# The second product turned: weights stationary, 512 tokens moving, output through 32x32 transposes

## The chip, the cores and the metric

The kernel runs on one core of one Trainium2 chip. A core has a matrix engine (TensorE, PE in the profile), a vector engine (VectorE, DVE), an activation engine (ScalarE, ACT), a general engine (GpSimd, POOL), a queue engine that here only issues transfers (SyncE, SP), and 16 DMA engines that the queues share. The metric is the device time of one execution in microseconds (us). Before the change, three runs took 592.19, 592.72 and 592.80 us; the median is 592.72 us.

## The reference, cut to what matters

There are two stages. The first is an attention block with 32 inducing points: for each of 4 batches of 12,480 tokens of width 128, the 32 points attend to the tokens and give `h` (32 x 128), and then every token attends to the 32 rows of `h`. The second is a two-layer network on the result, with a leaky unit between the layers whose slope is given per hidden channel.

```python
def mab(q, kv):
    s = scale * (q @ kv.transpose(0, 2, 1))
    s = s - s.max(-1, keepdims=True)
    a = np.exp(s)
    a /= a.sum(-1, keepdims=True) + 1e-09
    return a @ kv
h = mab(I, x)            # 4 x 32 x 128
x = mab(x, h)            # 4 x 12480 x 128
h = x @ w_in             # 49920 x 2048
g = np.maximum(h, 0.0) + alpha * np.minimum(h, 0.0)
out = g @ w_out          # 49920 x 128
```

## The kernel before, in words

The kernel never forms the attention output. For a batch it computes `hW = h @ w_in` once (32 x 2048). The hidden layer of a token is then `hW` weighted by the token's 32 exponentials, divided by their sum; since the leaky unit commutes with a positive factor, the division is left to the very end. The leaky unit is written as alpha times its input, which is linear, plus (1 - alpha) times the positive part. The linear part is folded into a 32 x 128 matrix `hA` per batch, and `W1` is `w_out` scaled by (1 - alpha).

*Groups and steps.* Tokens are worked in groups of 512 (`GRP`), four groups (`NQ`) to a stretch of 2,048 tokens, six stretches (`NS`) and a short group of 192 to a batch: 25 groups a batch, 100 in all. A group has four steps `j` (the short group two). In a step `fill` (L424) makes four matmuls, each with 32 rows of `hW` as weights and 512 columns of `rep` (the exponentials) moving; the four use different row groups of the array. Each writes one of six PSUM banks (`ring`). The four banks are evicted with a ReLU to `gt` in bf16 by ScalarE (L448) or VectorE (L450). Which engine takes which bank is fixed in advance by `make_plan` (L703), a beam search over a simple cost model, with 57 ns for each matmul of 128 columns. One step later `mm2` (L454) multiplies: for each bank and each of its four blocks of 128 tokens, a matmul has the block of `gt` as weights (128 x 128) and the matching 128 columns of `W1` moving, and adds to one of two accumulators `acc` (tokens on partitions, channels in the free dimension). The linear part is added to the accumulators of two groups at a time by `linear` (L479), eight matmuls of 128 columns with `rep` as weights.

*Output.* After a group's last step `finish` (L491) multiplies the accumulator with the reciprocal of each token's sum of exponentials (`rd`; one value per partition and block) on VectorE, from PSUM into `ob`, and stores `ob` with one DMA from the GpSimd queue (L516; the last groups from SP). Tokens are laid out so that each partition stores 2 KB in a row. `ob` has three buffers.

*What feeds it.* `b_scores` (L355) computes a stretch's exponentials `e2` (32 inducing points x 4 groups on 128 partitions) and stores them to DRAM (`e2d`); `b_rep` (L374) loads them back four times, as `rep`, on the partitions that `fill` reads. `b_den` (L394) sums them by four matmuls with `pick` and takes the reciprocal `rd`. For the next batch, `a_load` (L122) loads x with a cast to bf16 from the GpSimd queue, `a_xpose` (L140) transposes it into `xT` by a DMA transpose from SP, `a_scores` (L263) computes the scores of the inducing points, and their exponentials `e1` go through a second DMA transpose (`e1T`) to `a_accum`.

*What sets the order.* Every instruction is pinned to program order on its engine (`pin`). Beside the steps of the groups, side work is put in slots (group, step) by `at` (from L654): for a stretch `s`, `b_scores` four groups ahead of its first group, `b_rep` three and `b_den` two groups ahead; for the next batch, a load every two groups, its transpose three groups later and its scores five groups later. DMA issues wait on their queue in program order too, so a waiting issue on SP or GpSimd holds up all that follow there.

Of the kernel before, what the change touches and what calls it, by code (L numbers as in the profile page):

```python
# [25 lines left out]
def kernel(  # L26
# [50 lines left out]
    head_pool = ctx.enter_context(tc.tile_pool(name="headp", bufs=3))  # L77
    rep_pool = ctx.enter_context(tc.tile_pool(name="repp", bufs=3))
    dram = ctx.enter_context(
        tc.tile_pool(name="e2d", bufs=3, space=bass.MemoryType.DRAM)  # L80
    )
    ob_pool = ctx.enter_context(tc.tile_pool(name="obp", bufs=3))
# [4 lines left out]
    accs = [psum.tile([P, NB, C], f32, name=f"acc{i}") for i in range(2)]  # L87
# [14 lines left out]
    def new_batch(b):  # L102
# [11 lines left out]
        st.rden = {}  # L114
        if b > 0:
            st.es = work.tile([P, NS + 1], f32, name="es", tag="es")
            st.hacc = work.tile([P, C], f32, name="hacc", tag="hacc")
            nc.vector.memset(st.es[:], 0.0)
            nc.vector.memset(st.hacc[:], 0.0)
# [102 lines left out]
    def warm(st, n=1):  # L222
        for _ in range(n):
            mm(
                accs[0][:, 1:, :].rearrange("p k c -> p (k c)"), ident[:],
# [128 lines left out]

    def b_scores(st, s):  # L355
        ps = bank()
        if s < NS:
            for q in range(NQ):
                mm(ps[32 * q : 32 * q + 32, :], st.hT, st.xT[:, s, q, :])
            e2 = work.tile([P, GRP], bf16, name="e2", tag="e2")  # L360
            pin(nc.scalar.activation(out=e2[:], in_=ps[:], func=EXP, scale=scale_of(st)))  # L361
            w = GRP
        else:
            mm(ps[0:M, :REM], st.hT, st.xTr[:].rearrange("c j p -> c (j p)"))
            e2 = work.tile([M, REM], bf16, name="e2r", tag="e2r")
            pin(nc.scalar.activation(out=e2[:], in_=ps[0:M, :REM], func=EXP, scale=scale_of(st, M)))
            w = REM
# [16 lines left out]
    def b_scores_pe(st, q):  # L384
        if q == 0:
            st.rep0 = rep_pool.tile([P, NQ, GRP], bf16, name="rep", tag="rep")
        ps = bank()
        mm(ps[:], st.hT4[:], st.xT[:, 0, q, :])
        pin(nc.scalar.activation(
            out=st.rep0[:, q, :], in_=ps[:], func=EXP, scale=scale_of(st)  # L390
# [3 lines left out]
    def b_den(st, s):  # L394
        e2 = st.e2.pop(s)
        ps = bank()
        if s < NS:
            for j in range(NB):
                mm(ps[:, j * NQ : (j + 1) * NQ], e2[:, j * P : (j + 1) * P], pick[:])
            rd = work.tile([P, NB, NQ], f32, name="rd", tag="rd")  # L400
            pin(nc.vector.reciprocal(
                out=rd[:].rearrange("p j q -> p (j q)"), in_=ps[:, : NB * NQ]
            ))
        else:
            for j in range(JR):
                mm(ps[:PR, j : j + 1], e2[:, j * PR : (j + 1) * PR], pick[0:M, 0:1])
            rd = work.tile([PR, JR, 1], f32, name="rdr", tag="rdr")
            pin(nc.vector.reciprocal(
                out=rd[:].rearrange("p j q -> p (j q)"), in_=ps[:PR, :JR]
            ))  # L410
        st.rden[s] = rd


# [40 lines left out]
    def mm2(st, g, j, gt):  # L454
        pp, nb, cp = shape_of(g)
        acc = accs[(st.b * NG + g) % 2]
        begun = (g % 2 == 1 and st.b + g > 1) or cp > 1
        for r in range(4):
            for i in range(cp):
                c = r * NJ + j * cp + i  # L460
                for k in range(nb):
                    k0 = (i * nb + k) * pp
                    mm(
                        acc[:pp, k, :], gt[:, r, k0 : k0 + pp], W1[:, c, :],
                        start=(j == 0 and r == 0 and i == 0 and k == 0 and not begun),
                        stop=False, skip_group_check=True,
                    )
# [11 lines left out]
    def linear(st, groups):  # L479
        for k in range(NB):  # L480
            for r, g in enumerate(groups):
                pp, nb, cp = shape_of(g)
                if k < nb:
                    mm(
                        accs[(st.b * NG + g) % 2][:pp, k, :],
                        st.rep[g][32 * r : 32 * r + 32, k * pp : (k + 1) * pp],
                        st.hA[32 * r : 32 * r + 32, :],
                        start=((r == 1 or cp > 1) and k == 0), stop=False, skip_group_check=True,
                    )

    def finish(st, g):  # L491
        pp, nb, _ = shape_of(g)
        acc = accs[(st.b * NG + g) % 2]
# [321 lines left out]
```

## Time and profile before

| | |
|---|---|
| median of three runs | 592.72 us |
| span of the profiled execution (first to last instruction) | 591.0 us |
| own time of the profiled execution | not listed beside its span; the median is 1.7 us above the span |
| TensorE busy | 578.7 us (98%) |
| VectorE busy | 517.7 us (88%) |
| ScalarE busy | 502.5 us (85%) |
| GpSimd busy | 84.9 us (14%) |
| DMA packets | 81,825, 70.10 MB, 119 GB/s over the span |
| second product, matmuls of 128 x 128 x 128 | 6,144, mean 220 ns from start to modelled end |
| output multiply on VectorE, 128 x 512 | 96, 681 ns |
| granted TensorE clock | 1.00 |

How to read it: a row of a group names the line of the code, the engine, the operation, output<-inputs, shape and count, then busy time and mean duration. Busy times of TensorE are made from modelled ends of pipelined matmuls, so 98% does not say that it streams 98% of the time; the starts in the timeline do. A timeline row gives the start, the duration of a run of like instructions and their number, and in brackets how long the engine was idle before and what ended it. In the views by stretch, each engine's busy time is followed by its number of instructions, and the last three numbers are the granted clock, the busy share of the 16 DMA engines and GB/s. Time of a GpSimd or SP transfer issue is the issue alone; the landing is listed apart.

### The profile page before, as it was taken

The page shows a single profiled execution, that of the slowest core. Times are in us where ns is not written, and L with a number is a line of the kernel's source. Part 1 is how long each engine was busy: PE and PEld are TensorE (multiplying, and loading weights), DVE is VectorE, ACT ScalarE, POOL GpSimd, SP SyncE. Part 2 cuts the span into 40 slices and gives each one's busy share as a digit, 9 for nine tenths or more (in the row PEclk, how much of TensorE's full clock was granted, in tenths as well). Part 3 has the DMA queues.
Part 4 walks back from the last instruction along what each step waited for, and adds up shares of the span by engine and source line. Part 5 has one row for each costly group of instructions (what it writes and reads, how often), then busy time and mean ns, then how long its engine had stood idle before and what let it go on. Part 6 is the DMA issues. An engine that isn't in the chain of part 4 may idle for free.

```text
span 591.0 us, 21769 instructions
## 1 busy us (share of the span) xinstructions
PE 578.7 (98%) x9218; PEld 434.2 (73%) x9219; DVE 517.7 (88%) x869; ACT 502.5 (85%) x988; POOL 84.9 (14%) x170
## 2 busy tenths in 40 slices
PE   5999999999999999999999999999999999999997
PEld 4677777777777777777777777777777777777776
DVE  3688998999889989998989899988988998998996
ACT  2579888888889988888888998888888988989987
POOL 6631111101011111110111111101101101101100
PEclk9999999999999999999999999999999999999999
DMA  9973978751237569953126597985122221221211
GB/s 198 210 174 90 177 149 163 154 140 55 86 87 165 125 128 185 171 137 92 60 83 142 121 163 129 185 159 131 59 70 80 89 93 54 92 91 56 94 47 62
DMA packets 81825, 70.10 MB, mean 119 GB/s; under 512 B 55440, under 2 KB 71072, under 8 KB 81728
## 3 DMA queue, kind: packets, MB, share of 16 engines
q0 software_dynamic: 12528, 38.51, 26.0%
q1 hardware_dynamic: 69056, 29.68, 25.0%
q8 instruction: 72, 1.18, 0.8%
q10 hardware_dynamic: 144, 0.52, 0.2%
q14 instruction: 25, 0.20, 0.1%
HBM read 40.20 MB, written 28.75 MB: 117 GB/s over the span
## 4 chain that ended last, share of the span: by engine, by line
PE 97%; DVE 1%; DMA 1%; ACT 1%; issue 0%; SPq 0%
PE acc L96 68%; PE ring L96 27%; PE ring L172 1%; DMA ind_f<-in_inducing_dram 1%; ACT gt L448 0%; DVE xT L178 0%; DVE gt L450 0%; DVE ob L503 0%; DVE xn L612 0%; ACT xT L180 0%; SPq L526 0%; ACT ob L507 0%; DVE hT L246 0%; DVE ind_b L562 0%; PE ring L565 0%
## 5 line engine op out<-in xcount | busy, mean ns | idle before, releaser
L448 ACT ACTIVATE gt<-ring 128x512 bf16<-128x512 f32 x899 | 469.5, 599 | 67.8 <-ACT gt L448 27.4
L450 DVE TENSOR_SCALAR gt<-ring 128x512 bf16<-128x512 f32 x669 | 435.1, 685 | 52.2 <-PE ring L96 37.8
L96 PE MATMUL acc<-W,gt 128*128 128x128 bf16 x6272 | 417.9, 220 | 0.2 <-DVE ob L503 0.2
L96 PEld LDWEIGHTS <-gt 128*128 128x128 bf16 x6272 | 352.4, 98 | 79.6 <-issue 76.8
L96 PE MATMUL ring<-rep,hW 32*128 32x512 bf16 (+1 forms) x1600 | 157.3, 379 | 0.0
L516 POOL DMA_DIRECT2D out_dram<-ob x96 | 51.8, 540 | 476.5 <-DVE ob L503 412.6
L96 PEld LDWEIGHTS <-hW 32*128 32x128 bf16 x1600 | 41.1, 91 | 41.6 <-issue 0.5
L503 DVE TENSOR_TENSOR ob<-acc,rd 128x512 f32<-128x512 f32 x96 | 65.4, 681 | 2.5 <-PE acc L96 2.5
L96 PE MATMUL acc<-hA,rep 32*128 32x128 bf16 x392 | 19.8, 214 | 0.0
L96 PEld LDWEIGHTS <-rep 32*128 32x128 bf16 x392 | 15.6, 93 | 5.6
L129 POOL DMA_DIRECT2D xn<-in_x_dram x28 | 15.3, 551 | 3.3 <-DMA xn<-in_x_dram 2.4
L197 ACT ACTIVATE e1t<-ring 128x256 bf16<-128x256 f32 (+1 forms) x13 | 4.8, 371 | 10.5 <-PE ring L96 10.4
L178 DVE COPY xT<-ring 128x1024 bf16<-128x1024 bf16 (+1 forms) x12 | 8.0, 669 | 5.2 <-PE ring L172 4.8
L361 ACT ACTIVATE e<-ring 128x512 bf16<-128x512 f32 x18 | 11.0, 612 | 0.0
L269 ACT ACTIVATE e<-ring 128x512 bf16<-128x512 f32 x18 | 10.9, 605 | 0.0
L96 PE MATMUL ring<-xT,hT 128*32 128x512 bf16 (+1 forms) x97 | 10.0, 389 | 0.0
L172 PE MATMUL ring<-ident,xn 128*128 128x128 bf16 x96 | 8.8, 249 | 0.9 <-DVE xn L612 0.9
L172 PEld LDWEIGHTS <-xn 128*128 128x128 bf16 x96 | 6.8, 112 | 1.0 <-DVE xn L612 1.0
L96 PEld LDWEIGHTS <-hT 128*32 128x32 bf16 (+1 forms) x122 | 3.7, 92 | 5.1 <-issue 2.6
L96 PE MATMUL ring<-xn,e1T 128*32 128x128 bf16 x288 | 7.4, 221 | 0.0
L96 PE MATMUL ring<-xT,IT 128*32 128x512 bf16 x72 | 7.2, 390 | 0.0
L565 PE MATMUL ring<-ident,ind_b 32*128 32x32 bf16 x1 | 0.2, 205 | 6.1 <-DVE ind_b L562 6.1
(87 smaller groups left out, 113.6 us busy)
## 6 DMA issues: line engine op xcount, KB each, us to landing
out_dram<-ob POOLq DMA_DIRECT2D x93, 256.0 KB, 2.9
rep<-e2d SPq DMA_DIRECT2D x92, 128.0 KB, 3.4
xn<-in_x_dram POOLq DMA_DIRECT2D x18, 512.0 KB, 6.7
e2d<-e SPq DMA_DIRECT2D x24, 128.0 KB, 2.0
xn<-in_x_dram POOLq DMA_DIRECT2D x10, 256.0 KB, 8.5
w_out_f<-in_moe_w_out_dram POOLq DMA_DIRECT2D x4, 256.0 KB, 11.1
out_dram<-ob SPq DMA_DIRECT2D x3, 256.0 KB, 2.3
xs<-in_x_dram ACTq DMA_DIRECT2D x1, 512.0 KB, 4.9
```

The costliest lines, as they stand in the source:

```text
L96: return pin(nc.tensor.matmul(o, lhsT, rhs, start=start, stop=stop, **kw))
L129: pin(nc.gpsimd.dma_start(out=xn[:, i * w : (i + 1) * w, :], in_=src[:, i * w : (i + 1) * w, :]))
L172: pin(nc.tensor.transpose(tp[:, k * P : (k + 1) * P], xn[:, q, j * C : (j + 1) * C], ident[:]))
L178: pin(nc.vector.tensor_copy(out=dst, in_=tp[:, :w]))
L197: pin(nc.scalar.activation(out=e1t[:pp, :nb, :].rearrange("p k m -> p (k m)"), in_=ps[:pp, : nb * M], func=EXP, scale=scale,))
L269: pin(nc.scalar.activation(out=e1[:], in_=ps[:], func=EXP, scale=scale, accum_out=st.es[:, u : u + 1]))
L361: pin(nc.scalar.activation(out=e2[:], in_=ps[:], func=EXP, scale=scale_of(st)))
L448: pin(nc.scalar.activation(out=gt[:, r, :w], in_=ps[:, :w], func=RELU))
L450: pin(nc.vector.tensor_relu(gt[:, r, :w], ps[:, :w]))
L503: pin(nc.vector.tensor_tensor(out=ob[:pp, :cut, :], in0=acc[:pp, :cut, :], in1=rbc, op=MULT))
L516: pin((nc.sync if ending else nc.gpsimd).dma_start(out=dst, in_=ob[:pp, :nb, :]))
L565: nc.tensor.transpose(itp[:, :M], ind_b[:], ident[:M, :M])
```

## The change

In the second product the operands swap places: `W1` (128 hidden x 128 channels) becomes the stationary operand and 512 tokens of `gt` move, so that a bank takes one matmul instead of four, and the accumulator holds channels on partitions and tokens in the free dimension. `linear` is turned in the same way. `finish` now has three parts: VectorE transposes the accumulator in blocks of 32 x 32 into `ot` (two buffers), GpSimd multiplies by the reciprocals into `ob`, and four DMAs, one for each quarter of the channels, store 32 partitions x 16 runs of 32 channels (128 bytes) each. The order of the tokens inside a group is permuted so that this comes out right: the Exp of `b_scores` and `b_scores_pe` reads PSUM in a permuted order (`turned`), and the scores take their tokens in another order (`tokens_of`). The reciprocals are needed on other partitions: `b_den` stores them to DRAM (`rt`) from SP, and a new task `b_turn` loads them four times as `rdT`, one group later. The last group is no longer split between VectorE and ScalarE. `make_plan` is unchanged.

```diff
-    accs = [psum.tile([P, NB, C], f32, name=f"acc{i}") for i in range(2)]
+    accs = [psum.tile([P, GRP], f32, name=f"acc{i}") for i in range(2)]
...
+    def tokens_of(st, s, q):
+        return st.xT[:, s].rearrange("c j (q p) -> c j q p", q=NQ)[:, :, q, :]
+
+    def turned(ap, n):
+        return ap.rearrange("p (j i t) -> p t j i", j=n, i=32)
...
+        pin(nc.scalar.activation(
+            out=e2[:].rearrange("p (t j i) -> p t j i", j=n, i=32),
+            in_=turned(ps[:pp, :w], n), func=EXP, scale=scale_of(st, pp),
+        ))
...
+        rt = dram.tile([pp, n, nq], f32, name="rt", tag="rt" if s < NS else "rtr")
+        pin(nc.sync.dma_start(out=rt[:], in_=rd[:]))
+        st.rt[s] = rt
+
+    def b_turn(st, s):
+        n, nq, pp = (NB, NQ, P) if s < NS else (JR, 1, PR)
+        rdT = rd_pool.tile(
+            [P, pp // 32, n * nq], f32, name="rdT", tag="rdT" if s < NS else "rdTr"
+        )
+        src = st.rt.pop(s)[:].rearrange("(m i) k q -> i m (k q)", i=32)
+        for a in range(4):
+            pin(nc.sync.dma_start(out=rdT[32 * a : 32 * a + 32], in_=src))
+        st.rden[s] = rdT[:].rearrange("p m (k q) -> p k m q", q=nq)
...
     def mm2(st, g, j, gt):
         pp, nb, cp = shape_of(g)
+        t = pp * nb
         acc = accs[(st.b * NG + g) % 2]
         for r in range(4):
             for i in range(cp):
                 c = r * NJ + j * cp + i
-                for k in range(nb):
-                    k0 = (i * nb + k) * pp
-                    mm(
-                        acc[:pp, k, :], gt[:, r, k0 : k0 + pp], W1[:, c, :],
-                        start=(j == 0 and r == 0 and i == 0 and k == 0 and not begun),
-                        stop=False, skip_group_check=True,
-                    )
+                mm(
+                    acc[:, :t], W1[:, c, :], gt[:, r, i * t : (i + 1) * t],
+                    start=(j == 0 and r == 0 and i == 0 and not begun),
+                    stop=False, skip_group_check=True,
+                )
...
     def linear(st, groups):
+        for r, g in enumerate(groups):
+            pp, nb, cp = shape_of(g)
+            t = pp * nb
+            mm(
+                accs[(st.b * NG + g) % 2][:, :t], st.hA[32 * r : 32 * r + 32, :],
+                st.rep[g][32 * r : 32 * r + 32, :t],
+                start=(r == 1 or cp > 1), stop=False, skip_group_check=True,
+            )
...
     def finish(st, g):
-        ob = ob_pool.tile([P, NB, C], f32, name="ob", tag="ob")
-        pin(nc.vector.tensor_tensor(
-            out=ob[:pp, :cut, :], in0=acc[:pp, :cut, :], in1=rbc, op=MULT
-        ))
+        ot = ot_pool.tile([P, GRP], f32, name="ot", tag="ot")
+        pin(nc.vector.transpose(out=ot[:, :t], in_=acc[:, :t]))
+        ob = ob_pool.tile([P, GRP], f32, name="ob", tag="ob")
+        pin(nc.gpsimd.tensor_tensor(
+            out=ob[:, :t].rearrange("p (k m c) -> p k m c", k=nb, c=32),
+            in0=ot[:, :t].rearrange("p (k m c) -> p k m c", k=nb, c=32),
+            in1=rbc, op=MULT,
+        ))
...
-            dst = out[t0 : t0 + SUP, :].rearrange("(p q j) c -> q p j c", q=NQ, j=nb)[q]
+            dst = out[t0 : t0 + SUP, :].rearrange(
+                "(i b q) (a k) -> q a i b k", b=t // 32, q=NQ, k=32)[q]
...
-        pin((nc.sync if ending else nc.gpsimd).dma_start(out=dst, in_=ob[:pp, :nb, :]))
+        for a in range(4):
+            pin((nc.sync if ending else nc.gpsimd).dma_start(
+                out=dst[a],
+                in_=ob[32 * a : 32 * a + 32, :t].rearrange("p (b k) -> p b k", k=32),
+            ))
...
     at(0, lambda: b_den(st, 0), 2, (130, "D", 250))
+    at(1, lambda: b_turn(st, 0), 0)
...
             at(g + 2, lambda b=b, s=s: b_den(states[b], s), 3, (130, "D", 250))
+            at(g + 3, lambda b=b, s=s: b_turn(states[b], s), 3 if s < NS else 1)
...
             at(k + 3, lambda n=n: b_den(states[n], 0), 1, (130, "D", 250))
+            at(k + 4, lambda n=n: b_turn(states[n], 0), 0)
```

## The prediction, made before the result was known

> **What bounds the kernel now.** I read the page's busy line and its chain first, then the busy times by stretch, then one steady step instruction by instruction, then the rows that the change will replace.
>
> ```profile
> PE 578.7 (98%) x9218; PEld 434.2 (73%) x9219; DVE 517.7 (88%) x869; ACT 502.5 (85%) x988; POOL 84.9 (14%) x170
> PE 97%; DVE 1%; DMA 1%; ACT 1%; issue 0%; SPq 0%
> ```
>
> 97% of the chain that ended last is TensorE. Its busy time is modelled, so the starts in the timeline must confirm it. Two whole steps near the end, TensorE alone:
>
> ```profile
> 581.33 0.40 PE L96 MATMUL ring<-rep,hW 32*128 32x512 bf16 x4
> 581.66 1.07 PE L96 MATMUL acc<-W,gt 128*128 128x128 bf16 x16
> 582.66 0.40 PE L96 MATMUL ring<-rep,hW 32*128 32x512 bf16 x4
> 582.99 1.07 PE L96 MATMUL acc<-W,gt 128*128 128x128 bf16 x16
> ```
>
> A step lasts 582.66 - 581.33 = 1.33 us: 0.33 from the four first-product matmuls to the sixteen of the second product, then 1.00 to the next four. The sixteen take 1.07 us to the end of the last, and one takes 0.22 (the page's mean), so their starts lie (1.07 - 0.22)/15 = 57 ns apart. They stream without gaps; the 1.00 us is 15 x 0.057 plus 0.15 after the last start. So TensorE's own work is the step. Is there room beside it?
>
> ```profile
> 303.37 2.57 ACT L448 ACTIVATE gt<-ring 128x512 bf16<-128x512 f32 x5 [0.40 <-PE ring L96]
> 304.83 1.29 DVE L450 TENSOR_SCALAR gt<-ring 128x512 bf16<-128x512 f32 x2
> ```
>
> Run one after another, evictions come every (2.57 - 0.60)/4 = 0.49 us on ScalarE and 1.29 - 0.69 = 0.60 on VectorE. With 899 of them, ScalarE is occupied 441 us plus 33 of other work (502.5 - 469.5), 80% of the span; VectorE with 669 evictions and 96 output multiplies 459 plus 17, 81%. They leave about 20%.
>
> **The change, part by part.** (1) *Second product.* Sixteen matmuls of 128 columns become four of 512. The trace has no full-array matmul of 512 in a row, but it has 384 with a weight load each:
>
> ```profile
> 25.80 0.50 PE L96 MATMUL acc<-xT,ident 128*128 128x384 bf16 x2
> 26.23 0.39 PE L96 MATMUL ring<-rep,hW 32*128 32x512 bf16 x2
> ```
>
> One such matmul takes 323 to 337 ns, so the starts are 0.17 apart, and the second start is 0.26 before the next fill, that is 0.17 plus about 0.09. The switch therefore costs the same 0.09 as behind the 128s (0.15 - 0.057). From 57 ns at 128 and 165 at 384, 512 columns cost about 216. New: 3 x 0.216 + 0.216 + 0.09 = 0.955 against 1.00: -0.043 us a step, x 384 full steps = -16.5 us. The eight steps of the short groups go from 1.00 to eight matmuls of 192 (84 ns each) plus 0.09 = 0.76: -2 us. Each weight load (98 ns) hides under the 216 of the matmul before it. The 0.33 before them stays: weights for the whole array still follow matmuls that use it by rows. The linear term's eight matmuls of 128 in two row groups become two of 512 side by side, 4 x 0.054 against 0.216: zero. Sum: -18.5 us.
>
> The Trainium skill (TensorE: Matmul & The Clock Gate, section Back-to-back issue gap) gives about 81 ns a matmul at 128 columns and 131 at 512 in a stream with weight loads. By that a step would lose 16 x 81 - 4 x 131 = 772 ns, an estimate of -296 us; this trace has 57 ns at 128, so I go by the trace.
>
> (2) *VectorE.* The multiply (681 ns x 96) is replaced by a 32x32 transpose of the same 128x512 f32 from PSUM. No transpose stands in the trace. Every VectorE operation of this shape that does costs 681 to 685, so I take about 700; its bound above is a transpose that streams half as fast, 1.2 us (the 0.53 us of streaming doubled). At 700 it fits into the 19% that is free. That is the cover; without it see rival 3.
>
> (3) *GpSimd* now holds a multiply and four store issues a group, in order, with the x loads between:
>
> ```profile
> L516 POOL DMA_DIRECT2D out_dram<-ob x96: 526/539/562, 40.4 to 571.2; - x96
> L547 POOL DMA_DIRECT2D w_out_f<-in_moe_w_out_dram x4: 747/753/769, 12.2 to 16.0; - x4
> L590 POOL TENSOR_TENSOR W<-w_out_f,om_al x4: 1042/1042/1047, 23.9 to 27.0; 128x512 bf16<-128x512 f32 x4
> ```
>
> (durations min/median/max). The multiply is like the W row: 1.04 us. Each store has 32 x 16 = 512 runs; the w_out load has 128 x 4 = 512 runs and issues in 753 ns, the old store with 128 runs in 539. Taking the row with as many runs: 1.04 + 4 x 0.753 + 0.15 (28 loads x 0.55 over 100 groups) = 4.2 us against a group of about 5.2 to 5.4. It fits, so zero; bounds 3.4 (539 each) and 7.4 us (if 128-byte runs cost four times the difference: 1.6 each). The multiply waits for the turned denominators, with VectorE behind it only when both transposed buffers are full, some 10 us later.
>
> (4) *DMA engines.* 2,048 runs of 128 B a group instead of 64 packets. The page's queue shares price them: q0 is 26.0% x 16 x 591 / 12528 = 196 ns a packet of 3 KB, q1 34 ns a packet of 430 B. From 22.9 to 25.9 us, where the w_out load lands, q0 moved 0.45 MB in 52.5% x 16 x 3.0 us, 29 ns per 512 B run. So a 128 B run lies between 7 (in proportion) and 29; I take 15, nearer to the small packets. Per group: 2048 x 15 / 16 = 1.9 us for 0.8 before, +22 points of DMA share.
>
> ```profile
> 55.00:120.00 65.00, 65.00 (x1038) 48.21 (x1035) 58.79 (x98) 57.50 (x116) 8.14 (x15) 1.00 0.80 157
> 120.00:175.00 55.00, 54.90 (x884) 41.11 (x882) 48.95 (x88) 47.20 (x94) 5.92 (x11) 1.00 0.29 83
> ```
>
> The share (second number from the right) is 0.80 while the next batch is loaded, 0.29 after it. Who feels it is the transposed x: it is issued at 105.21 and scored at 113.44,
>
> ```profile
> 105.21 3.31 SPq L143 DMA_TRANSPOSE xT<-xn  x1
> 113.44 0.40 PE L96 MATMUL ring<-xT,IT 128*32 128x512 bf16 x4
> DMA to landing us min/median/max: 4.7/6.5/7.9
> ```
>
> 8.2 us in which the landing takes 6.5, at worst 7.9. Stores that take 1.1 us more, and two groups that are 0.35 shorter, leave about 0.5; I charge 18 transposes with 0.2 each, +4 us (0 to 23, the last if a run costs 29 ns: 2.9 us later each, 1.3 beyond the slack). TensorE waits there, and behind it the next fill.
>
> The skill speaks against this part: DMA: Bandwidth & Descriptors, section Specifications, asks for 512 B or more a transfer and says that smaller ones are read, modified and written. An estimate by it, each run at the price of 512 B, would be the +23 end. No run here shows such a store yet.
>
> (5) *SP.* Per four groups one store of the denominators and four loads more, 5 x 0.43 (the issue time of the rep loads) = 2.1 us of 21; they stand behind the x transpose, and the multiply that needs them has some 5 us to spare: zero, bound +4 if they hold up the rep loads. The permuted Exp reads and token views change no counts: zero, bounds -1 and +8 (28 Exps at double time, half of it hidden).
>
> (6) *End.* The last output was a 0.29 us multiply and 0.36 on ScalarE, then one store. Now: transpose (0.4), GpSimd multiply (0.5), four SP stores in a row behind four others: three more issues of 0.43, and +0.3 for the hop. With the loads of the last denominators behind the previous stores, +3 (2 to 6).
>
> Sum on the profiled execution's span: 591.0 - 18.5 + 4 + 3 = 579.5. The span stands 1.7 below the median of the runs (592.72), so 581; I say 582, since evictions in a shorter step wait now and then (1 us).
>
> **Rivals.** (1) *GpSimd becomes the bound.* For it: five instructions in order where one was. Against: the 753 ns row. It decides from (5.3 - 1.04 - 0.15)/4 = 1.03 us an issue. At 1.2 us a group takes 6.0: 39 us to the first output + 99 x 6.0 + 3 = 636. (2) *DMA engines bound the load stretches.* 55 to 120, 175 to 260 and 320 to 405 have share 0.74 to 0.82; at 29 ns the new stores add 2.9 us a group, 55 points, a share of 1.35. If only the transposes feel it: 579.5 - 4 + 23 + 1.7 = 600; if the stretches stretch, 235 us x 0.35 = +80, about 655. Against: landing times may hide more than shares say. (3) *The transpose streams at half rate.* VectorE then has 6.7 x 0.60 + 1.2 + 0.17 = 5.4 us a group, TensorE's gain is lost: 592 to 596. (4) *The shorter step is not used*, since TensorE now waits for evictions as placed by a plan that still reckons 57 ns a matmul: 589 to 593. For it: VectorE and ScalarE look 85 to 88% busy; against: occupied 80%.
>
> **How the numbers follow.** My forecast 0.50 (its own range 574 to 590), rival 1 0.17, rival 2 0.18, rival 3 0.07, rival 4 0.08. The range of 573 to 640 leaves out the upper halves of rivals 1 and 2 and a little below, 0.16. The measurement can tell 0.2% (1.2 us). Faster: 0.46 of my own case and 0.04 of the others; the same 0.04; slower 0.46.
>
> **What would show it.** Right: second-product matmuls in fours 0.216 apart, step 1.29; VectorE transposes near 0.70; GpSimd issues near 0.75 and its total near 400 us; DMA share near 1.0 while loading; TensorE's waits at the scores of x. Wrong: GpSimd busy throughout with VectorE's transpose waiting for its multiply (rival 1), stores landing more than 10 us after issue (rival 2), transposes of 1.2 us (rival 3), TensorE's fill waiting for gt evictions (rival 4).

## The result and the profile after

The changed kernel takes 588.58 us (median of 8 runs, 586.38 to 591.21) against 592.65 us (8 runs, 592.01 to 594.34) of the kernel before on the same chip: a ratio of 0.9932, interval 0.9913 to 0.9952. That is 4.1 us less, where 10.7 were forecast. The profiled execution is the longest of the eight, 591.21 us with a span of 589.4; differences inside it are read against the span of 591.0 before.

First the page's busy line and the engines' shares of the chain that ended last:

```profile
PE 558.5 (95%) x4185; PEld 196.4 (33%) x4255; DVE 517.6 (88%) x869; ACT 502.0 (85%) x987; POOL 384.8 (65%) x558
POOL 42%; issue 24%; PE 20%; DMA 9%; SPq 3%; ACT 0%; POOLq 0%; DVE 0%
```

TensorE has fallen from 98% to 95% busy, GpSimd risen from 14% to 65%. The chain now puts 42% on GpSimd. That looks like rival 1; the experiments show that it is not. The chain is followed back from the last instruction, here a store behind GpSimd's last multiply, and a queue whose instructions follow one another closely holds such a walk fast.

A steady step near the end, TensorE alone, from the timeline:

```profile
573.47 0.40 PE L98 MATMUL ring<-rep,hW 32*128 32x512 bf16 x4
573.80 1.04 PE L98 MATMUL acc<-gt,W 128*128 128x512 bf16 x4
574.77 0.40 PE L98 MATMUL ring<-rep,hW 32*128 32x512 bf16 x4
```

A step lasts 574.77 - 573.47 = 1.30 us, the second product 574.77 - 573.80 = 0.97 of it. It was 1.00 before, and the forecast had 0.955. In the trace's single records the starts of the four lie 226, 216 and 216 ns apart, and the next fill starts 312 ns after the last: the first gap is 10 ns longer than the other two, and the switch back to the fill costs 312 - 216 = 96 ns.

Groups of instructions of the page (line, engine, operation, count | busy, mean ns | idle before and what ended it):

```profile
L531 POOL DMA_DIRECT2D out_dram<-ob x384 | 245.8, 668 | 35.6 <-POOL ob L518 29.7
L518 POOL TENSOR_TENSOR ob<-ot,rdT 128x512 f32<-128x512 f32 (+1 forms) x100 | 105.5, 1055 | 152.9 <-DVE ot L516 146.3
L516 DVE STREAM_TRANSPOSE ot<-acc 128x512 f32<-128x512 f32 (+1 forms) x100 | 69.4, 694 | 3.8 <-PE acc L98 3.8
L98 PE MATMUL ring<-xT,IT 128*32 128x512 bf16 x72 | 7.4, 401 | 3.9 <-DMA xT<-xn 3.9
```

The VectorE transpose costs about what the multiply cost. A group on GpSimd costs 1.07 + 0.30 (the wait of the first store for the multiply) + 4 x 0.67 + 0.17 for the x loads = 4.2 us, the figure of the forecast. The idle time in the last row is new (0.0 before): TensorE waits for the transposed x. The waits (sum in us, number, longest), then the busy times by stretch around the longest of them (clock, DMA share and GB/s last):

```profile
PE ring L98 <- DMA xT<-xn: 3.9, 6, 2.3
```

```profile
250.00:252.00 2.00, 0.80 (x7) 0.10 (x4) 1.57 (x5) 1.08 (x2) 1.63 (x3) 1.00 1.12 250
252.00:254.00 2.00, 0.62 (x4) 0.24 (x6) 0.19 (x1) 0.18 (x1) 0.00 (x0) 0.68 1.07 256
254.00:256.00 2.00, 1.91 (x7) 0.41 (x6) 0.00 (x0) 0.50 (x2) 0.00 (x0) 0.50 0.55 132
256.00:258.00 2.00, 2.00 (x15) 0.74 (x12) 1.81 (x3) 1.79 (x4) 0.42 (x1) 0.96 0.54 106
```

A wait of 2.3 us costs more than itself. The granted clock falls to 0.50 while TensorE still waits and stays there for some 3.4 us ((0.32 + 0.50 + 0.04) x 2 us / 0.50, from the last three rows), so the matmuls up to 256 run at half speed. Two steps take 6.6 us here (250.41 to 257.05), and the same two 2.9 us in `e3_xpose_early` below, which has no wait: of the 3.7 us between them 2.3 are the wait and most of the rest is the clock.

And the end, the last TensorE row of before first, then the changed kernel:

```profile
585.65 2.01 PE L96 MATMUL acc<-W,gt 128*96 128x128 bf16 x32
```

```profile
576.42 3.44 SPq L531 DMA_DIRECT2D out_dram<-ob  x4
578.96 1.88 PE L98 MATMUL acc<-gt,W 128*128 128x192 bf16 x16
579.97 1.97 SPq L430 DMA_DIRECT2D rdT<-rt  x4
580.95 0.38 DVE L516 STREAM_TRANSPOSE ot<-acc 128x192 f32<-128x192 f32 x1 [1.00 <-PE acc L98]
582.03 5.21 SPq L531 DMA_DIRECT2D out_dram<-ob  x8
583.35 0.51 POOL L518 TENSOR_TENSOR ob<-ot,rdT 128x192 f32<-128x192 f32 x1 [2.69 <-DMA rdT<-rt]
```

TensorE's last matmul ends at 580.84, 6.8 us earlier than before (587.66). The span ends 8.6 us after it, where it was 3.3: 5.3 of the 6.8 are given back. The loads of the last denominators (`rdT`) stand on SP behind the stores of an earlier group, the last multiply waits 2.69 us for them, and then eight stores go out one after another at 0.65 us.

### The profile page after: what moved, and what is told of

Its sections match the earlier page's. It is cut to its first block, busy times and chain, and to the rows that moved or that the text cites. A ratio compares the mean times of both kernels' runs of the same rounds, so it can differ in the third digit from the quotient of the medians.

```text
span 589.4 us, 12415 instructions
## 1 busy us (share of the span) xinstructions
PE 558.5 (95%) x4185; PEld 196.4 (33%) x4255; DVE 517.6 (88%) x869; ACT 502.0 (85%) x987; POOL 384.8 (65%) x558
## 4 chain that ended last, share of the span: by engine, by line
POOL 42%; issue 24%; PE 20%; DMA 9%; SPq 3%; ACT 0%; POOLq 0%; DVE 0%
POOL out_dram L531 28%; PE acc L98 13%; POOL ob L518 13%; PE ring L98 6%; DMA xT<-xn 3%; DMA xn<-in_x_dram 3%; DMA rdT<-rt 2%; POOL xn L132 1%; SPq L430 1%; SPq L146 1%; SPq L531 1%; DMA out_dram<-ob 0%; ACT gt L466 0%; DMA rt<-rd 0%; POOLq L531 0%
## 5 line engine op out<-in xcount | busy, mean ns | idle before, releaser
L98 PE MATMUL acc<-gt,W 128*128 128x512 bf16 x1530 | 391.2, 376 | 10.1 <-issue 8.9
L531 POOL DMA_DIRECT2D out_dram<-ob x384 | 245.8, 668 | 35.6 <-POOL ob L518 29.7
L518 POOL TENSOR_TENSOR ob<-ot,rdT 128x512 f32<-128x512 f32 (+1 forms) x100 | 105.5, 1055 | 152.9 <-DVE ot L516 146.3
L98 PEld LDWEIGHTS <-W 128*128 128x128 bf16 x1600 | 124.7, 98 | 173.1 <-issue 80.0
L98 PE MATMUL ring<-rep,hW 32*128 32x512 bf16 (+1 forms) x1600 | 159.1, 379 | 0.0
L516 DVE STREAM_TRANSPOSE ot<-acc 128x512 f32<-128x512 f32 (+1 forms) x100 | 69.4, 694 | 3.8 <-PE acc L98 3.8
L98 PE MATMUL acc<-rep,hA 32*128 32x512 bf16 (+1 forms) x100 | 19.3, 369 | 0.0
L132 POOL DMA_DIRECT2D xn<-in_x_dram x28 | 17.5, 634 | 2.6 <-DMA xn<-in_x_dram 1.8
L98 PEld LDWEIGHTS <-hT 128*32 128x32 bf16 (+1 forms) x122 | 3.7, 92 | 12.3 <-issue 12.2
L98 PEld LDWEIGHTS <-e 128*128 128x128 bf16 x96 | 4.0, 96 | 9.4 <-issue 9.4
## 6 DMA issues: line engine op xcount, KB each, us to landing
w_out_f<-in_moe_w_out_dram POOLq DMA_DIRECT2D x4, 256.0 KB, 11.2
```

The lines of the kernel that those rows point to most:

```text
L98: return pin(nc.tensor.matmul(o, lhsT, rhs, start=start, stop=stop, **kw))
L132: pin(nc.gpsimd.dma_start(out=xn[:, i * w : (i + 1) * w, :], in_=src[:, i * w : (i + 1) * w, :]))
L516: pin(nc.vector.transpose(out=ot[:, :t], in_=acc[:, :t]))
L518: pin(nc.gpsimd.tensor_tensor(out=ob[:, :t].rearrange("p (k m c) -> p k m c", k=nb, c=32), in0=ot[:, :t].rearrange("p (k m c) -> p k m c", ...
L531: pin((nc.sync if ending else nc.gpsimd).dma_start(out=dst[a], in_=ob[32 * a : 32 * a + 32, :t].rearrange("p (b k) -> p b k", k=32),))
```

## The experiments

All times are medians beside the kernel before on the same chip (592.35 to 592.68 us).

### The shorter step alone

`e1_pe_only` turns the second product and the linear term and leaves multiply, stores and denominators as before:

```diff
-                for k in range(nb):
-                    k0 = (i * nb + k) * pp
-                    mm(
-                        acc[:pp, k, :], gt[:, r, k0 : k0 + pp], W1[:, c, :],
+                mm(
+                    acc[:, :t], W1[:, c, :], gt[:, r, i * t : (i + 1) * t],
```

> The kernel before with the turned second product and linear term alone; the multiply, the denominators and the 2 KB stores stay as before, so the output has tokens and channels mixed up and is not the reference's. Theory A (the gain on TensorE is real but smaller than forecast, 30 ns a step as the starts in the changed profile show, and the rest was lost at the x transposes and at the end): 384 x 0.030 + 2 for the short groups = 13.5 us less than before, 579 us, give or take 1.5. The size in the prediction (43 ns a step): 574. Rival B (a shorter step is not used, since TensorE waits for evictions placed by a plan that reckons the old step): 587 to 590, with TensorE's fills waiting for gt evictions.

580.35 us, ratio 0.9795 (0.978 to 0.9809): 12.2 us less. 30 ns x 384 steps are 11.5 us, and the six short steps that the trace shows between two fills went from 1.03 to 0.77 us, 1.6 us more. So all but some 0.9 us of the shorter step is used, rival 4 (589 to 593) falls, and the worth of the step was 12, not 18.5. What the rest of the change costs is 588.58 - 580.35 = 8.2 us.

### Run length, denominators, and the number of stores

`e2_runs_2k` keeps the four stores of a group, each with runs of 2 KB:

```diff
-                out=dst[a],
-                in_=ob[32 * a : 32 * a + 32, :t].rearrange("p (b k) -> p b k", k=32),
+                out=run[32 * a : 32 * a + 32], in_=ob[32 * a : 32 * a + 32, :t],
```

> The changed kernel, still with four stores a group, but each stores 32 partitions x one run of 2 KB (768 B for the short groups) where 16 runs of 128 B went; the values land at wrong places of the output. Theory A (the 128-byte runs load the DMA engines and delay the x transposes): the waits of some 4.5 us at the scores go, and the issues on SP at the end get shorter: 582 to 584. Rival C (the waits come from the rt and rdT transfers that were added on SP, not from the run length): 586 to 588. Rival D (GpSimd's queue holds the kernel): the issues fall from 0.67 towards 0.54, about 50 us less on GpSimd, and the time falls by more than 8, below 580.

587.45 us, 1.1 less than the changed kernel. Its issue rows:

```profile
PE 559.0 (95%) x4185; PEld 196.9 (34%) x4255; DVE 517.4 (88%) x869; ACT 502.1 (86%) x987; POOL 331.8 (57%) x558
L536 POOL DMA_DIRECT2D out_dram<-ob x384 | 193.4, 509 | 38.5 <-POOL ob L518 27.9
```

GpSimd is relieved of 53 us and the time hardly moves: GpSimd is not the bound, whatever the chain says. Waits for `xT` remain (two in this trace, 2.3 us on TensorE), so they come without 128-byte runs too. The 1.1 us lie inside the scatter of its runs (585.03 to 589.26), and the end alone got shorter by as much (7.2 us after TensorE's last matmul instead of 8.6).

`e7_no_turn` takes the store and the loads of the denominators away for the full stretches:

```diff
+        if s < NS:
+            st.rden[s] = rd
+            return
         rt = dram.tile([pp, n, nq], f32, name="rt", tag="rt" if s < NS else "rtr")
```

> The changed kernel without the trip of the denominators through DRAM for the full stretches: GpSimd multiplies by the reciprocals as they lie on the partitions before the turn, which are those of other tokens, so the output is not the reference's; 120 transfers fewer on SP. Theory C (those transfers delay the x transposes): the waits at the scores go, 584.5 to 585.5. Theory E (the later loads do): 587.5 to 589, with the waits as they were.

587.99 us, and six waits for `xT` are still there (3.0 us on TensorE). SP's five extra transfers a stretch are not the cause.

`e13_eight` splits each store in two, to find where GpSimd does become the bound:

```diff
+            for lo in ((0,) if ending else (0, h)):
+                    out=dst[a][:, lo:hi], in_=src[:, lo:hi],
```

> The changed kernel with eight stores a group in place of four, each of half the runs (256 of 128 bytes). Rival 1 of the prediction put the point from which GpSimd sets the pace at 1.03 us for each of four issues, 4.1 us a group. An issue of 32 runs took 0.50 to 0.54 us and one of 512 runs 0.67, so one of 256 about 0.59: 8 x 0.59 + 1.07 + 0.15 = 5.9 us a group against 5.2 on TensorE, 39 + 99 x 5.9 + 4 = 627 to 635 us, GpSimd busy throughout and VectorE's transposes waiting for its multiply. If the issues of the traced kernel are partly waiting and not work (a ring that is full), the same runs in more issues cost less than that: under 610.

668.26 us (2 runs), ratio 1.1279 (1.1256 to 1.1301). One group on GpSimd, from the timeline, and the wait that marks the bound:

```profile
450.30 1.09 POOL L518 TENSOR_TENSOR ob<-ot,rdT 128x512 f32<-128x512 f32 x1
451.68 4.63 POOL L535 DMA_DIRECT2D out_dram<-ob  x8 [0.30 <-POOL ob L518]
```

```profile
DVE ot L516 <- POOL ob L518: 89.2, 80, 3.7
```

This is what rival 1 looks like: VectorE's transposes wait for GpSimd's multiply 80 times. In the changed kernel that wait is absent. The mean issue is 0.587 us as reckoned; the expectation was some 35 us short, most of it the 0.30 us hop in each group that it left out (30 us). The point from which GpSimd decides is therefore, as an estimate, (5.2 - 1.07 - 0.30 - 0.17) / 4 = 0.92 us an issue rather than 1.03; this run, with 8 x 0.587 us, lies well beyond it. At 4 x 0.67 there is room.

### What makes the transposed x late

`e3_xpose_early` issues the transposes a group earlier:

```diff
-                at(k + 3, lambda n=n, u=u: a_xpose(states[n], u))
+                at(k + 2, lambda n=n, u=u: a_xpose(states[n], u))
```

> The changed kernel with one number changed: the DMA transpose of the next batch's x goes two groups after its load, not three, so it has one group (5.2 us) more before its scores. Theory A: the waits for xT at the scores (4 to 5 us in the profiled run) go, 584 to 585, and the granted clock stays at 1.00. Rivals B and D (evictions or GpSimd hold it): 588 to 589, since another wait takes their place.

585.07 us (584.91 to 585.27), ratio 0.9871 (0.9855 to 0.9888), no wait for `xT`. So the waits and their clock cost 3.5 us. TensorE's last matmuls here, then in `e1_pe_only`:

```profile
573.36 1.88 PE L98 MATMUL acc<-gt,W 128*128 128x192 bf16 x16
```

```profile
573.43 1.88 PE L96 MATMUL acc<-gt,W 128*128 128x192 bf16 x16
```

With the waits gone TensorE is done as early as in the kernel that has none of the new output (575.24 and 575.31 us). So VectorE's transpose, GpSimd's multiply and the new stores cost TensorE nothing else, and the 585.07 - 580.35 = 4.7 us that are left are the end: 8.2 us from the last matmul to the end of the span, where `e1_pe_only` has 3.3.

But why do the transposes land later than before? The next runs move the load of x on GpSimd's queue. `e6_load_first` puts it ahead of the multiply and the stores:

```diff
-            at(base, begin)
+            at(base, begin, 0)
-                at(k, lambda n=n, u=u: a_load(states[n], u))
+                at(k, lambda n=n, u=u: a_load(states[n], u), 0)
```

> The changed kernel with the loads of the next batch's x put one step earlier, so that on GpSimd's queue a load goes ahead of the multiply and four stores of the group before and not behind them; nothing else moves (the load was issued 3.2 us later in the changed kernel than in the run with the turned product alone: 78.02 against 74.78 us for the same unit). Theory E (the x transposes land late because the loads, 3 us later, now run beside them): the waits for xT at the scores go, 584.5 to 585.5, as in the run with the earlier transpose. Theory C (they land late because of the rt and rdT transfers on SP): 587.5 to 589.

592.89 us (11 runs, 586.92 to 594.31): slower, not faster. `e11_load_first2` is the same kernel, traced again:

> The changed kernel with the loads of x put ahead of the multiply and the stores on GpSimd's queue, a second time, for the trace of a longer execution: the earlier runs lay between 587 and 594 us and the traced one was the shortest. If the time is lost at the scores of x, waits of TensorE for the transposed x of 5 us and more in sum; if GpSimd's multiply holds the accumulators up, waits of VectorE's transposes on the multiply and of TensorE on VectorE; if neither is there, steps that are longer throughout, with a lower granted clock.

591.9 us. Only one transpose is waited for, the first:

```profile
43.82 3.10 SPq L146 DMA_TRANSPOSE xT<-xn  x1
43.89 0.65 POOL L132 DMA_DIRECT2D xn<-in_x_dram  x1
...
58.67 0.40 PE L98 MATMUL ring<-xT,IT 128*32 128x512 bf16 x4 [3.74 <-DMA xT<-xn]
```

A load of another part of x was issued 0.07 us after the transpose, and the transpose took until 58.6 to land, 14.8 us (12.3 in the first trace, at 586.92 us). `e10_all` joins this with the earlier transposes and the shorter end below:

> The changed kernel with all three: transposes of x a group earlier, the loads of x ahead of the multiply on GpSimd's queue, and the shorter end. Without the second the time was 583.2 us, with no wait for the transposed x left. If putting the load first does harm by itself (it moves the multiply that frees the transposed buffers): 586 to 590. If its harm came through the transposes of x, which now have a group more: 583 again.

607.18 us (593.46 to 624.76): neither forecast. The four runs scatter over 31 us, so the median sizes nothing; the trace, of a run of 608.33 us, shows where its time went. Four pairs met within 0.4 us, and two of them were waited for; the first, in the timeline and by stretch:

```profile
83.96 5.09 SPq L146 DMA_TRANSPOSE xT<-xn  x1
84.11 0.68 POOL L132 DMA_DIRECT2D xn<-in_x_dram  x1
...
109.51 0.62 PE L98 MATMUL ring<-xT,IT 128*32 128x512 bf16 x4 [9.49 <-DMA xT<-xn]
```

```profile
96.00:107.00 11.00, 3.87 (x30) 1.16 (x28) 4.94 (x9) 4.87 (x10) 0.00 (x0) 0.83 1.34 80
```

The load landed at 107.1 and the transpose at 109.5, 23 and 25 us after issue, where 6 to 8 are usual. In the 11 us from 96 to 107 the packets' busy share is 1.34 and only 80 GB/s move, as if the packets were open and waited for each other. That gave theory F: a transpose lands the later, the nearer a load of x is issued to it. Before, the load stood 5.8 us ahead of the transpose at 105.21 that the prediction shows:

```profile
99.43 0.56 POOL L129 DMA_DIRECT2D xn<-in_x_dram  x1
```

In the changed kernel the load comes behind a multiply and four stores:

```profile
101.81 0.62 POOL L132 DMA_DIRECT2D xn<-in_x_dram  x1
103.99 5.12 SPq L146 DMA_TRANSPOSE xT<-xn  x1
112.38 0.40 PE L98 MATMUL ring<-xT,IT 128*32 128x512 bf16 x4 [0.39 <-DMA xT<-xn]
```

2.2 us ahead; and the issue itself takes SP 5.12 us, where it took 3.31. To set this distance and nothing else, I went back to the kernel with only the product turned. `e12_late_load` moved the load two steps on in program order:

```diff
-                at(k, lambda n=n, u=u: a_load(states[n], u))
+                at(k, lambda n=n, u=u: a_load(states[n], u), 3)
```

> The kernel with only the second product turned (old multiply, old store; output mixed up), and in it the loads of x moved two steps later in their group, from step 1 to step 3, some 2.6 us, which is about as late as the fuller GpSimd queue made them in the changed kernel. Nothing else of the change is in it. Theory E (a load issued later runs beside the transpose of the other unit and both land late; that is where the changed kernel's 4 us at the scores of x come from): waits for the transposed x appear at the scores, 3 to 4 us in sum, 583 to 584.5 us. Rival (the lateness needs the four stores a group, in number or in traffic): 580.4 us as without the move, at most one wait.

580.25 us, and it tells nothing: the load stands 5.09 us ahead of the transpose here as in `e1_pe_only` (75.49 and 80.58, 74.78 and 79.87 there), since in both places the next thing ahead of it on the queue is the same store. A place in program order is not a time. `e14_delay3` and `e15_delay5` delay the load by idle multiplies instead (three or five):

```diff
     def a_load(st, u, pieces=1):
+        for _ in range(3 if st.b else 0):
+            pin(nc.gpsimd.tensor_tensor(out=pad[2][:], in0=pad[0][:], in1=pad[1][:], op=MULT))
```

> The kernel with only the second product turned (old multiply, old store; output mixed up), and ahead of each of the 28 minus 10 later loads of x three multiplies of 128x512 on GpSimd, on tiles that nothing else uses, 3.1 us. This delays the loads and adds no transfer. Without it the loads were issued 5.1 to 5.5 us ahead of the transposes of the other unit, which landed 5 to 9 us after issue; with it 2.0 to 2.4 us ahead, as in the changed kernel. Theory F (a transpose of x lands the later the nearer in time a load of x is issued): landings of 7 to 10 us, TensorE waits for xT at 4 and more of the 18 scores, 583 to 585 us. Rival (the lateness needs the traffic or the number of the new stores): landings as before, 580.4 us, at most one wait.

> The same with five multiplies ahead of each load, 5.2 us, so that load and transpose are issued within half a microsecond of each other. Theory F, with the five such pairs in the kernels that put the load first (landings of 12 to 26 us): landings of 10 us and more at most of the pairs, waits of 3 us and more each at the scores, 595 to 650 us and a wide scatter. If only the order of the two matters, and not that they meet: 583 to 585 us, as with three. Rival: 580.4 us.

With three, 588.28 us (ratio 0.992, 0.9903 to 0.9936), 7.9 us slower than without; with five, 580.37 (0.9799, 0.9785 to 0.9814), as without. A multiply took 1.33 us here, not 1.04, so the distances came out other than planned. Three, then five:

```profile
101.61 3.98 POOL L130 TENSOR_TENSOR pad<-pad,pad 128x512 f32<-128x512 f32 x3
...
105.52 0.58 POOL L136 DMA_DIRECT2D xn<-in_x_dram  x1
106.88 5.97 SPq L150 DMA_TRANSPOSE xT<-xn  x1
...
116.03 0.40 PE L98 MATMUL ring<-xT,IT 128*32 128x512 bf16 x4 [0.71 <-DMA xT<-xn]
```

```profile
97.76 6.67 POOL L130 TENSOR_TENSOR pad<-pad,pad 128x512 f32<-128x512 f32 x5
...
103.04 1.95 SPq L150 DMA_TRANSPOSE xT<-xn  x1
104.37 0.58 POOL L136 DMA_DIRECT2D xn<-in_x_dram  x1
111.40 0.40 PE L98 MATMUL ring<-xT,IT 128*32 128x512 bf16 x4
```

With the load 1.4 us ahead, the issue takes 5.97 us, and six scores wait:

```profile
PE ring L98 <- DMA xT<-xn: 6.0, 6, 2.1
```

With the load 1.3 us behind, the issue takes 1.95 us and nothing waits. No store was added or cut up in either. So the distance alone can make the lateness, and it is one-sided in these two runs: with a load 1.2 to 2.0 us ahead a transpose landed after 8.2 to 10.7 us, with one 2.5 and 2.9 us ahead after 6.8 and 6.5, and with one 1.0 to 2.2 us behind after 4.3 to 6.8. The expectation that five multiplies would be worst was wrong, since the pairs didn't meet.

Is it the whole cause in the changed kernel? `e16_after_delay3` puts the three idle multiplies into the changed kernel:

```diff
     def a_load(st, u, pieces=1):
+        for _ in range(3 if st.b else 0):
+            pin(nc.gpsimd.tensor_tensor(out=pad[2][:], in0=pad[0][:], in1=pad[1][:], op=MULT))
```

> The changed kernel whole, and ahead of each later load of x three idle multiplies of 128x512 on GpSimd, 3.2 us. In the changed kernel the loads were issued 1.8 to 2.9 us ahead of the transposes of the other unit; with this they come 0.3 to 1.4 us behind them, and later still where GpSimd falls behind (two groups and a load then take it 11.2 us of 10.5). Theory F as the last two runs left it (a load 0 to 3 us ahead of a transpose makes it land late, one that comes a microsecond behind does not): no waits for xT at the scores, 584 to 586 us although the kernel does more. If the new stores take part in the lateness: waits remain, 588 to 592 us. If GpSimd's lag reaches the transposed buffers: VectorE's transposes wait on the multiply, 590 us and more.

601.26 us, ratio 1.0142 (1.0125 to 1.0159): a miss. GpSimd fell behind in the load stretches, the loads came so late that 12 of the 18 transposes were issued within 0.3 us of the landing of their own load, and seven scores waited 11.2 us. It doesn't answer the question. `e17_load_first_i2` sets the distance the other way round, without added work:

```diff
-                at(k, lambda n=n, u=u: a_load(states[n], u))
+                at(k, lambda n=n, u=u: a_load(states[n], u), 0 if i > 1 else 1)
```

> The changed kernel with the loads of x ahead of the multiply and the stores on GpSimd's queue, as in the two runs that put the load first, but only from the third load of a batch on; the first two stay where they were. In those two runs 17 of 18 transposes had a load some 4 us behind them or none near and landed in 4.3 to 9.1 us without a wait; only the first of the whole program met its load within 0.4 us, landed after 12.2 and 14.8 us and was waited for. The new stores and the places of the transposes are untouched. Theory F: no wait for xT, 584.5 to 586 us, little scatter, as with the transposes a group earlier (585.1). If the new stores take part by themselves, or putting the load first harms in another way: 587 us and more, scattered as before.

586.77 us (586.48 to 589.82), ratio 0.9923 (0.9895 to 0.9952). The trace has no wait for `xT` left, with the stores and the places of the transposes unchanged: the distance is the cause of the waits in the changed kernel as well. It isn't all of the lateness there, since two transposes with a load 1.4 us behind them landed after 7.9 and 8.5 us, where `e15_delay5` had 4.3 to 6.8; the new stores may take part in that. The time lies between the two forecasts, 1.8 us below the changed kernel and 1.7 above `e3_xpose_early`. Of those 1.7 us the traces show 1.3 (586.48 against 585.21): none at the scores of x, 0.1 ahead of the first fill, 0.5 at the end, and 0.7 in one step in which a fill waits for `rep`:

```profile
443.35 0.38 PE L98 MATMUL ring<-rep,hW 32*128 32x512 bf16 x1 [0.47 <-DMA rep<-e2d]
```

Why `rep` comes late there stays open.

### The end

`e4_tail` loads the last denominators a group earlier and gives half the stores of the last two groups to ScalarE's queue; `e8_tail2` does the first and spreads the last group's stores alone over ScalarE and GpSimd:

```diff
-            pin((nc.sync if ending else nc.gpsimd).dma_start(
+            last2 = ending and g >= NG - 2 and a % 2 == 1
+            pin((nc.scalar if last2 else nc.sync if ending else nc.gpsimd).dma_start(
...
-            at(g + 2, lambda b=b, s=s: b_den(states[b], s), 3, (130, "D", 250))
-            at(g + 3, lambda b=b, s=s: b_turn(states[b], s), 3 if s < NS else 1)
+            d = 1 if (b, s) == (B - 1, NS) else 0
+            at(g + 2 - d, lambda b=b, s=s: b_den(states[b], s), 3, (130, "D", 250))
+            at(g + 3 - d, lambda b=b, s=s: b_turn(states[b], s), 3 if s < NS or d else 1)
```

> The changed kernel with another end: the last stretch's denominators are summed and turned one group earlier, and the last two groups' stores go half from SP and half from ACT, which is idle by then. Theory A (from TensorE's last matmul to the end 8.6 us pass where 3.3 did before, because the last multiply waits for rdT behind the stores of the group before, and eight stores of 0.65 us stand in a row on one queue): 3 to 4.5 us less, 584 to 585.5. If the end is bound by the landing alone: less than 1 us.

588.85 us, no gain:

```profile
578.12 1.53 ACTq L532 DMA_DIRECT2D out_dram<-ob  x2
...
580.30 1.56 PE L98 MATMUL acc<-gt,W 128*128 128x192 bf16 x8 [3.07 <-ACT gt L466]
581.97 0.38 DVE L516 STREAM_TRANSPOSE ot<-acc 128x192 f32<-128x192 f32 x1 [4.59 <-PE acc L98]
```

The two stores of the last group but one stood on ScalarE ahead of the last evictions and waited there for GpSimd's multiply, and TensorE waited 3.07 us for those evictions: the last accumulator came 1.0 us later than in the changed kernel's trace, though TensorE had been 2.6 us ahead of it until then. In `e8_tail2` only stores with nothing behind them are moved:

```diff
+            final = (st.b, g) == (B - 1, NG - 1)
+            q_of = nc.scalar if final and a % 2 else nc.gpsimd if final else nc.sync
```

> The changed kernel with another end: the last denominators are summed and turned one group earlier, as in the run that split the last stores, but only the very last group's stores leave SP, half to ACT, which has nothing left to evict then, and half to GpSimd. Theory A (the end waits for rdT and then for eight stores in a row on SP): from TensorE's last matmul to the end 4.5 to 5 us where 8.6 passed, 584 to 585.5. If the queue order is not what holds the end: 588 to 589.

587.09 us; from TensorE's last matmul to the end of the span 5.9 us instead of 8.6. `e9_best` joins it with the earlier transposes:

> The earlier x transpose and the new end together. If the two losses are separate and theory A holds for both: 588.6 - 3.5 - 4 = 581, between 580 and 582.5. If the end cannot be shortened: 585.

583.20 us (583.01 to 583.56), ratio 0.9845 (0.983 to 0.9859), which beats both kernels. Its end:

```profile
569.46 1.77 SPq L430 DMA_DIRECT2D rdT<-rt  x4
571.46 6.80 SPq L533 DMA_DIRECT2D out_dram<-ob  x8
576.40 0.51 POOL L518 TENSOR_TENSOR ob<-ot,rdT 128x192 f32<-128x192 f32 x1 [0.75 <-DVE ot L516]
576.94 1.59 ACTq L533 DMA_DIRECT2D out_dram<-ob  x2
577.87 1.12 POOL L533 DMA_DIRECT2D out_dram<-ob  x2 [0.96 <-POOL ob L518]
```

The multiply waits for its transpose only.

## Why the prediction was right or wrong

The sign was right, and 588.6 us lies inside the range; the size was off by more than half. In steps:

- *(1) Second product, -18.5 us.* This step failed, as a term that was mis-sized: -12.2 measured alone. The 216 ns between matmuls was right (with some luck: a straight line through the forecast's 57 ns at 128 and 165 at 384 gives 219). Missed were the first gap's surplus of 10 ns and 6 ns of the switch back (96 for my 90), so that the stretch is 0.970 us and not 0.955. Both stood in the single starts of the trace of before: a first gap of 66 ns, then 56, and 152 from the last start to the next fill. Each is about 1% of the stretch, but the gain is a difference of two nearly equal stretches: the step went from 1.327 to 1.297 us, 30 ns and not 43, and 13 ns in 384 steps are 5 us. The remaining 1.3 us are short groups that gained a little less than 2 us and some 0.9 us of the shorter step that is not used.
- *The rule weighed there.* Going by the trace was right: the 131 ns at 512 columns of the Trainium skill (TensorE: Matmul & The Clock Gate, section Back-to-back issue gap) is not what this stream with a weight load for each matmul shows (216). The 215.7 ns that Part 1 of the same page gives for a warm array agrees.
- *(2) VectorE, 0.* Right: 694 ns in the mean of all transposes, 707 in that of the 96 full ones, against 681 for the multiply. Rival 3 falls.
- *(3) GpSimd, 0.* Right: 4.2 us a group, and issues of 0.67 us against 0.75 from the row of w_out. Rival 1 falls for this kernel and is real where the queue gets fuller (`e13_eight`), by the estimate above from some 0.92 us an issue.
- *(4) DMA, +4.* The size came out right, 3.5 (`e3_xpose_early`), and the place too, the scores of x, but the size is luck, since the reason was wrong. A run of 128 B costs about 10 ns where the stores have queue q0 to themselves (from 430 to 550 us it is busy 22.3% x 16 x 120 us for 85 stores of 512 runs), less than the 15 assumed, and with runs of 2 KB waits remain. The load of x is pushed behind four store issues and a multiply on GpSimd and comes to lie 2 us ahead of a transpose. I had costed GpSimd's fuller queue by its sum and not by what stands behind it. Rival 2 falls: the DMA share in the load stretches (55 to 120, 175 to 260, 320 to 405 us) rose from 0.80, 0.74 and 0.82 to 0.92, 0.87 and 0.83, and with the waits at the scores gone TensorE lost nothing (`e3_xpose_early`).
- The Trainium skill's rule on 512 bytes (DMA: Bandwidth & Descriptors, section Specifications: shorter transfers are read, modified and written) costs this kernel next to nothing: the same stretch of `e2_runs_2k` has q0 busy 19.5% instead of 22.3%, and the time fell by 1.1 us, inside the scatter of its runs.
- *(5) SP, 0.* Right: `e7_no_turn` gains 0.6, inside the scatter.
- *(6) End, +3.* Mis-sized: +5.3 in the trace and 4.7 by the medians of `e3_xpose_early` and `e1_pe_only`, though inside its own 2 to 6. A store issue of this form costs 0.65 us on SP, not 0.43, and the wait of the last multiply for its denominators, named but without a price of its own, was 2.69.
- *Slips that decide nothing.* In (1), 1.00 - 0.955 is 0.045, where 0.043 was entered; in (3), issues of 1.6 us give an upper bound of 7.6 us, not 7.4; in (4), the figures named leave 8.2 - 0.35 - 1.1 - 6.5 = 0.25 us, not 0.5.

The account, from the runs: 592.6 - 12.2 (`e1_pe_only`) + 3.5 (`e3_xpose_early`) + 5.3 (the end in the trace) = 589.2, measured 588.6. From the side of the forecast: 582 + 6.3 (second product) + 2.3 (end) - 0.5 (scores) - 1 (waiting evictions, which the 12.2 already holds) = 589.1.

## What to carry to other kernels

When a change puts more instructions on a queue, cost not only their sum but each thing that now stands behind them, and look where that thing lands in time beside transfers of the other queues; a load that is delayed by some four microseconds (`e14_delay3`) can hurt where a delay of nearly seven does not (`e15_delay5`). Where a gain is the difference of two stretches that are nearly equal, take both from the single starts in the trace, not from rows rounded to hundredths. At the end of a kernel, put only such issues on a busy engine's queue as have nothing behind them.

## What the runs showed of the hardware that was not expected

- A DMA transpose (SP) and a cast load (GpSimd) of 512 KB disturb each other by distance and order: landing after 4.3 to 6.8 us with the load 1.0 us or more behind in `e15_delay5`, 8.2 to 10.7 with it 1.2 to 2.0 us ahead in `e14_delay3`, 12 to 26 within half a microsecond in the runs that put the load first, in one of these pairs at a busy share of 1.34 and 80 GB/s. Why is not shown; that the transpose's issue on SP grows from 1.95 to 5.97 us says that it is held up while it is still being issued.
- With a wait of 2.3 us TensorE's granted clock went to 0.50 for some 3.4 us. Waits of 1.8 us (`e2_runs_2k`) and 2.1 us (`e14_delay3`) brought it too, one of 2.53 us in `e16_after_delay3` did not. The Trainium skill (TensorE: Matmul & The Clock Gate, Part 1) asks for an idle window of about 3.4 us before the clock halves; here less was enough, and the length of the wait alone did not decide it.
- The cost of a store issue on GpSimd grows little with its runs: 0.51 us with 32 (`e2_runs_2k`), 0.587 with 256 (`e13_eight`), 0.668 with 512 (the changed kernel).
